# Linear attention and a two-layer network on one core: the query maxima cross the partition groups through a DRAM tile, per token half, where copies within on-chip memory did it per head pair

## The chip, the cores and the metric

The kernel runs on one core of a Trainium2 chip. The metric is device time in microseconds (us) of one execution. The kernel before has a median of 1189.84 us over three runs (1189.03 to 1190.34).

The core has five engines, each with its own queue of instructions that it takes strictly in order: TensorE (PE; its weight loads are listed as PEld), VectorE (DVE), ScalarE (ACT), GpSimd (POOL) and SyncE (SP), which here only issues DMAs. An instruction that waits holds up all that stands behind it on its engine.

## The reference

```python
def phi(x):
    proj = np.einsum('bhsd,df->bhsf', x, w_phi)
    proj = proj - np.max(np.abs(proj), axis=-1, keepdims=True)
    return np.concatenate([np.exp(proj), np.exp(-proj)], axis=-1)
q_p, k_p = (phi(q), phi(k))
kv = np.einsum('bhsf,bhsd->bhfd', k_p, v)
z = np.sum(k_p, axis=2)
num = np.einsum('bhsf,bhfd->bhsd', q_p, kv)
den = np.einsum('bhsf,bhf->bhs', q_p, z)[..., None] + 1e-06
attn = num / den
...
h = x @ w_in            # x: (4608, 512), the attention's output, heads side by side
out = np.maximum(0.01 * h, h) @ w_out
```

There are 8 batches, 8 heads, 576 tokens of 64 numbers; `w_phi` is 64 x 128; the network goes from 512 to 2048 and back. What the change touches is the `max(abs(proj))` of the queries: one number for each token and head, over 128 features.

## The kernel before, in words

**Attention.** Two heads make a pair, and 32 pairs (8 batches of 4) are worked one after the other. The first four have code of their own that the change leaves alone. For the others, `k_phase(i)` makes the 128 x 64 key-value sums of pair i and `q_phase(i)` uses them. Pairs 4 to 7 work in plain float32 (`nat`); from pair 8 on each operand is split into a rounded part and a rest, and each product is made of two or three matmuls. The text below calls `q_phase(i)` "phase i".

**A query phase** handles the pair's 576 tokens in two halves of 288 (u = 0, 1):

- L362 to L365: for each head the projection is made with the features on the 128 partitions and the tokens along the row, in a PSUM tile `a`.
- L366: a DVE transpose in blocks of 32 x 32 moves it to the tile `tq`. Within each block tokens are now on partitions and features along the row. The four partition groups of 32 hold four quarters of the features.
- L368: a reduction gives each partition the maximum over its 32 features, for 18 blocks (2 heads x 9 blocks of 32 tokens). This is a quarter maximum; four of them, 32 partitions apart, must still be joined. This is done after both halves are there: L370 issues three DMAs that copy the groups 1 to 3 to the first 32 partitions (tile `m`), L373 reduces the four, and L375 issues three DMAs that copy the result `mx` back to the groups 1 to 3.
- L381 subtracts the maximum (once per half), L383 transposes back in blocks to `mb` (features on partitions again), L388 and L389 take exp of plus and minus the value on ACT, and L395 and a POOL operation of L72 split it into `qh` and `ql`.
- L404, L406 and L409 are the matmuls with the key-value sums. ACT moves numerator and denominator out (L411, L412; denominator in `dn`), L415 to L419 bring the reciprocals into place on DVE, and POOL multiplies (L421) in the tile `ring`, which holds two batches.

**The network** runs over 18 blocks of 256 tokens. `layer1` (L595, L596, L598) makes a slice of 128 hidden features in the PSUM tile `h`; ACT applies the slope (L602) and rounds (L67), POOL makes the rest (L72); `layer2` (L615 to L617) adds the slice to two PSUM tiles `acc`. At a block's end DVE or ACT copies it out and SP stores it (L623). A block can start only when all heads of its tokens are in `ring`. `load_weights` prepares the network's weights on ACT and DVE (L172 to L186) in the first fifth of the run.

**What sets the order.** The code only states priorities. Attention has a higher priority than the network's steps, so a list scheduler puts an attention instruction into an engine's queue as soon as it holds it to be ready, and fills the rest with the network's matmuls. The scheduler's result is a fixed order per engine. A tile takes a buffer of its tag's pool when one is free: `mb` has one, `dn` has two, `tq` has one. DMAs are issued by SP in its order; an issue waits there until its data are ready and its target is free.

Of the kernel before, what the change touches and what calls it, by code (L numbers as in the profile page):

```python
# [9 lines left out]
F32 = mybir.dt.float32  # L10
# [4 lines left out]
ALU = mybir.AluOpType  # L15
AX = mybir.AxisListType

P = 128
# [3 lines left out]
U = 288  # L22
# [22 lines left out]
def attention_moe_kernel(ctx: ExitStack, tc: tile.TileContext, q, k, v, vt, w_phi, w_in, w_out, out):  # L45
    nc = tc.nc
    cp = ctx.enter_context(tc.tile_pool(name="cp", bufs=1))
    sp = ctx.enter_context(tc.tile_pool(name="sp", bufs=1))
    ps = ctx.enter_context(tc.tile_pool(name="ps", bufs=1, space=bass.MemoryType.PSUM))

    def ct(shape, dt, name):
        return cp.tile(shape, dt, tag=name, name=name)

    def st(shape, dt, tag, name=None):
        return sp.tile(shape, dt, tag=tag, name=name or tag, bufs=BUFS.get(tag, 1))
# [18 lines left out]
    def pt(tag):  # L74
        return ps.tile([P, 512], F32, tag=tag, name=tag, bufs=PBUFS[tag])
# [259 lines left out]
    def blocks(x):  # L335
        return x.rearrange("p a b -> p (a b)").rearrange("p (c d) -> p c d", d=32)

    def q_phase(i):
# [13 lines left out]
            wq = w_phi_split()  # L352
            wq_h, wq_l = wq[:, 0], wq[:, 1]
        tq = st([P, 2, 2, U], F32, "tq")
        m = st([P, 4, 2, 18], F32, "mb", "m")
        for u in range(2):
            us = slice(U * u, U * u + U)
            for j in range(2):
                pq = pt("a")[:, 0:U]
                if nat:  # L360
                    r = slice(64 * j, 64 * j + 64)
                    nc.tensor.matmul(pq, lhsT=bd[r, F * j : F * j + F], rhs=rq[r, us], start=True, stop=True)  # L362
                else:
                    nc.tensor.matmul(pq, lhsT=wq_h, rhs=qs[:, j, us], start=True, stop=False)  # L364
                    nc.tensor.matmul(pq, lhsT=wq_l, rhs=qs[:, j, us], start=False, stop=True)  # L365
                nc.vector.transpose(tq[:, u, j], pq)  # L366
                yield
            nc.vector.tensor_reduce(m[:, 0, u], blocks(tq[:, u]), axis=AX.X, op=ALU.max, apply_absolute_value=True)  # L368
        for a in range(1, 4):
            nc.sync.dma_start(m[0:32, a], m[32 * a : 32 * a + 32, 0])  # L370
        yield
        mx = st([P, 2, 18], F32, "mx")
        nc.vector.tensor_reduce(mx[0:32], m[0:32].rearrange("p a u c -> p u c a"), axis=AX.X, op=ALU.max)  # L373
        for a in range(1, 4):
            nc.sync.dma_start(mx[32 * a : 32 * a + 32], mx[0:32])  # L375
        yield
        kvh, kvl = kvs_of[i]
        for u in range(2):
            us = slice(U * u, U * u + U)
            tu = blocks(tq[:, u])  # L380
            nc.vector.tensor_tensor(tu, tu, mx[:, u].unsqueeze(2).broadcast_to([P, 18, 32]), op=ALU.subtract)  # L381
            mb = st([P, 2, U], F32, "mb")
            nc.vector.transpose(mb.rearrange("p a b -> p (a b)"), tq[:, u].rearrange("p a b -> p (a b)"))  # L383
            yield
# [14 lines left out]
            dn = st([P, U], F32, "dn")  # L399
# [158 lines left out]
    def attention():  # L558
        for i in range(NP, B * NP + 1):
            gens = [k_phase(i)] if i < B * NP else []  # L560
            if i > NP:
                gens.append(q_phase(i - 1))
            if i == NN:
                for _ in range(5):
                    next(gens[1])
                    yield i - 1
            while gens:
                for it in list(gens):
                    if next(it, end) is end:
                        gens.remove(it)  # L570
                    else:
                        yield i - 1
            yield i
# [137 lines left out]
```

## Time and profile before

| | us |
|---|---|
| median of three runs | 1189.84 |
| the profiled execution, its own time | 1187.94 |
| its span, first to last instruction | 1186.2 |
| PE busy in it | 1153.7 (97%) |
| DVE busy | 769.2 (65%) |
| ACT busy | 861.3 (73%) |
| POOL busy | 632.7 (53%) |

The page of the profile gives for each group of instructions the line, the engine, the operation, the tiles it writes and reads, the count, the busy time and the mean length, then the idle time of the engine just before them and what ended it. A view of waits lists "who <- whom: us in total, times, longest". A timeline gives the start, the length and the instruction. Views of windows give the busy time of each engine in a stretch. All times in them are from the start of the span. The granted clock of PE was 1.00 throughout.

### The profile page before, as it was taken

How to read it: one execution, taken by the hardware profiler on the slowest of the kernel's cores; microseconds unless marked ns; L12 is line 12 of the kernel's file. 1: busy time of each engine (PE TensorE's matmuls, PEld its weight loads, DVE VectorE, ACT ScalarE, POOL GpSimd, SP SyncE). 2: the span in 40 equal slices, each digit the busy share in tenths (PEclk: the TensorE clock that was granted, in tenths of full speed). 3: DMA queues.
4: the chain of work that ended last, by engine and by line, in shares of the span. 5: the costliest groups of instructions: out<-in, count | busy, mean ns of one | idle time of the engine just before them, and what ended most of it. 6: DMA issues, size and time to landing. Idle time of an engine off the chain costs nothing.

```text
span 1186.2 us, 21604 instructions
## 1 busy us (share of the span) xinstructions
PE 1153.7 (97%) x7496; PEld 1026.5 (87%) x7496; DVE 769.2 (65%) x1326; ACT 861.3 (73%) x2266; POOL 632.7 (53%) x709
## 2 busy tenths in 40 slices
PE   8899999899998999999999999999999999999998
PEld 5677778799887989889999999999999989899997
DVE  5988995587788778777777777757777765200000
ACT  5978775878788778777888878868887785433232
POOL 0131222576576667666666666757666666433232
PEclk9999999999999999999999999999999999999999
DMA  8436331211111111111111111101111100000000
GB/s 218 135 91 168 103 108 36 70 41 34 51 33 50 34 34 29 42 34 30 52 33 51 33 51 26 48 23 40 33 50 34 40 3 20 1 19 9 10 19 18
DMA packets 71005, 57.88 MB, mean 49 GB/s; under 512 B 53232, under 2 KB 54512, under 8 KB 70896
## 3 DMA queue, kind: packets, MB, share of 16 engines
q1 hardware_dynamic: 70896, 56.51, 17.1%
q8 instruction: 59, 0.97, 0.3%
q14 instruction: 50, 0.41, 0.1%
HBM read 46.27 MB, written 9.44 MB: 47 GB/s over the span
## 4 chain that ended last, share of the span: by engine, by line
PE 47%; DVE 2%; DMA 1%; issue 0%; ACT 0%; POOL 0%; SPq 0%; DVEq 0%; ACTq 0%; POOLq 0%
PE h L598 6%; PE h L596 6%; PE h L595 6%; PE acc L616 6%; PE acc L617 6%; PE acc L615 6%; PE c L228 3%; PE a L409 1%; PE a L404 1%; PE a L406 1%; PE a L251 1%; PE a L365 1%; PE a L364 1%; DVE tq L381 0%; DMA mx<-mx 0%
## 5 line engine op out<-in xcount | busy, mean ns | idle before, releaser
L72 POOL TENSOR_TENSOR gl<-g,gh 128x256 fp32r<-128x256 f32 x288 | 237.3, 827 | 305.4 <-ACT gh L67 220.2
L595 PE MATMUL h<-xh,w0h 128*128 128x256 f32 x1088 | 278.8, 283 | 2.4 <-ACT xh L67 1.3
L596 PE MATMUL h<-xh,w0l 128*128 128x256 f32 x1088 | 276.6, 281 | 0.0
L595 PEld LDWEIGHTS h<-xh,w0h 128*128 128x128 f32 x1088 | 205.4, 189 | 12.4 <-ACT g L602 2.4
L615 PE MATMUL acc<-w1h,gh 128*128 128x512 f32 x544 | 214.3, 394 | 0.2 <-DVE o L69 0.2
L616 PE MATMUL acc<-w1l,gh 128*128 128x512 f32 x544 | 213.3, 392 | 0.0
L596 PEld LDWEIGHTS h<-xh,w0l 128*128 128x128 f32 x1088 | 205.3, 189 | 8.4 <-issue 0.4
L617 PE MATMUL acc<-w1h,gl 128*128 128x512 f32 x544 | 203.5, 395 | 2.6 <-POOL rv L198 1.2
L598 PE MATMUL h<-xl,w0h 128*128 128x256 f32 x1088 | 191.2, 281 | 0.0
L602 ACT ACTIVATE g<-h 128x256 f32<-128x256 f32 x288 | 108.3, 381 | 106.0 <-PE h L598 83.0
L72 POOL TENSOR_TENSOR ql<-eq,qh 128x576 fp32r<-128x576 f32 x96 | 142.9, 1500 | 53.3 <-DVE qh L395 44.3
L67 ACT CAST gh<-g 128x256 fp32r<-128x256 f32 x288 | 115.2, 403 | 63.0 <-PE acc L616 60.9
L598 PEld LDWEIGHTS h<-xl,w0h 128*128 128x128 f32 x1088 | 155.9, 188 | 0.9 <-issue 0.4
L72 POOL TENSOR_TENSOR kpl<-ek,kph 128x512 fp32r<-128x512 f32 x72 | 101.5, 1410 | 75.9 <-ACT kph L67 59.3
L617 PEld LDWEIGHTS acc<-w1h,gl 128*128 128x128 f32 x544 | 99.5, 188 | 19.5 <-POOL rv L198 1.4
L69 DVE COPY o<-acc 128x512 f32<-128x512 f32 x17 | 11.7, 688 | 161.0 <-DMA out_dram<-o 118.0
L615 PEld LDWEIGHTS acc<-w1h,gh 128*128 128x128 f32 x544 | 102.5, 188 | 12.1 <-DVE o L69 0.4
L616 PEld LDWEIGHTS acc<-w1l,gh 128*128 128x128 f32 x544 | 102.3, 188 | 11.7
L282 ACT ACTIVATE ek<-pmk,m 128x128 f32<-128x128 f32 (+1 forms) x240 | 89.5, 390 | 13.5 <-DVE m L259 13.1
L281 ACT ACTIVATE ek<-pmk,m4n 128x128 f32<-128x128 f32 (+1 forms) x240 | 90.1, 392 | 8.6 <-DVE m4n L265 3.9
L395 DVE TENSOR_REDUCE qh<-eq 128x576 fp32r<-128x576 f32 x96 | 69.0, 751 | 25.7 <-ACT eq L389 22.9
L256 DVE TENSOR_TENSOR pmk<-a,pmk 128x256 f32<-128x256 f32 (+1 forms) x120 | 49.6, 420 | 54.0 <-ACT pmk L67 52.0
(183 smaller groups left out, 2404.8 us busy)
## 6 DMA issues: line engine op xcount, KB each, us to landing
out_dram<-o SPq DMA_DIRECT2D x36, 256.0 KB, 2.1
rq<-in_q_dram SPq DMA_DIRECT2D x28, 288.0 KB, 2.9
rk<-in_k_dram SPq DMA_DIRECT2D x27, 288.0 KB, 2.8
rv<-in_v_dram SPq DMA_DIRECT2D x29, 256.0 KB, 3.5
ring<-in_w_in_dram SPq DMA_DIRECT2D x9, 512.0 KB, 3.7
f<-in_w_out_dram SPq DMA_DIRECT2D x7, 512.0 KB, 3.6
f<-in_w_in_dram SPq DMA_DIRECT2D x7, 512.0 KB, 3.6
ring<-in_w_out_dram SPq DMA_DIRECT2D x5, 512.0 KB, 3.8
```

The source lines that it names most:

```text
L67: nc.scalar.copy(o, i)
L72: (nc.vector if pick(key) == "v" else nc.gpsimd).tensor_tensor(o, a, b, op=op)
L281: nc.scalar.activation(ek[r, j, 0:F], pmk[r, h], AF.Exp, bias=m4n[r, h : h + 1])
L282: nc.scalar.activation(ek[r, j, F:256], pmk[r, h], AF.Exp, scale=-1.0, bias=m4[r, h : h + 1])
L395: nc.vector.tensor_reduce(qh, eq.unsqueeze(3), axis=AX.X, op=ALU.max)
L595: nc.tensor.matmul(ph, lhsT=weight(0, "h", ft)[:, d * P : d * P + P], rhs=xh[d], start=d == 0, stop=False)
L596: nc.tensor.matmul(ph, lhsT=weight(0, "l", ft)[:, d * P : d * P + P], rhs=xh[d], start=False, stop=False)
L598: nc.tensor.matmul(ph, lhsT=weight(0, "h", ft)[:, d * P : d * P + P], rhs=xl[d], start=False, stop=d == NP - 1)
L602: nc.scalar.activation(g, ph, AF.Prelu, alpha=0.01)
L615: nc.tensor.matmul(a, lhsT=gh[:, ts], rhs=weight(1, "h", ft), start=ft == 0, stop=False)
L616: nc.tensor.matmul(a, lhsT=gh[:, ts], rhs=weight(1, "l", ft), start=False, stop=False)
L617: nc.tensor.matmul(a, lhsT=gl[:, ts], rhs=weight(1, "h", ft), start=False, stop=ft == NFT - 1)
```

## The change

Each half of a phase now joins its own quarter maxima. The half's reduction (now L372) writes 18 numbers per partition to a tile `mu`, which takes a buffer of the tag `dn`. One DMA (L374) writes them to a DRAM tile `md` of 256 rows of 18 numbers, twice: rows 0 to 127 and again rows 128 to 255. A second DMA (L375) reads them back so that partition p gets the rows p, p + 32, p + 64 and p + 96, side by side; these reads overlap each other. A reduction over the four (L383) then runs on all 128 partitions, in the loop over the halves, just ahead of the subtraction (L384). The three DMAs each way, the reduction on 32 partitions and the tile `mx` are gone. DMAs per phase: four in place of six; joining reductions on DVE: two in place of one. The read waits on SP for the write to land.

```diff
+    dp = ctx.enter_context(tc.tile_pool(name="dp", bufs=1, space=bass.MemoryType.DRAM))
...
-        m = st([P, 4, 2, 18], F32, "mb", "m")
+        m = []
         for u in range(2):
...
-            nc.vector.tensor_reduce(m[:, 0, u], blocks(tq[:, u]), axis=AX.X, op=ALU.max, apply_absolute_value=True)
-        for a in range(1, 4):
-            nc.sync.dma_start(m[0:32, a], m[32 * a : 32 * a + 32, 0])
-        yield
-        mx = st([P, 2, 18], F32, "mx")
-        nc.vector.tensor_reduce(mx[0:32], m[0:32].rearrange("p a u c -> p u c a"), axis=AX.X, op=ALU.max)
-        for a in range(1, 4):
-            nc.sync.dma_start(mx[32 * a : 32 * a + 32], mx[0:32])
+            mu = st([P, U], F32, "dn", "m")
+            mx, mr = mu[:, 0:18], mu[:, 36:108].rearrange("p (a c) -> p a c", c=18)
+            nc.vector.tensor_reduce(mx, blocks(tq[:, u]), axis=AX.X, op=ALU.max, apply_absolute_value=True)
+            md = dp.tile([8 * 32, 18], F32, tag="md", name="md", bufs=4)
+            nc.sync.dma_start(md.rearrange("(r p) c -> p r c", r=2), mx.unsqueeze(1).broadcast_to([P, 2, 18]))
+            nc.sync.dma_start(mr, bass.AP(md.tensor, md.offset, [[18, P], [32 * 18, 4], [1, 18]]))
+            m.append(mu)
         yield
         kvh, kvl = kvs_of[i]
         for u in range(2):
             us = slice(U * u, U * u + U)
             tu = blocks(tq[:, u])
-            nc.vector.tensor_tensor(tu, tu, mx[:, u].unsqueeze(2).broadcast_to([P, 18, 32]), op=ALU.subtract)
+            mt, mr = m[u][:, 18:36], m[u][:, 36:108]
+            nc.vector.tensor_reduce(mt, mr.rearrange("p (a c) -> p c a", c=18), axis=AX.X, op=ALU.max)
+            nc.vector.tensor_tensor(tu, tu, mt.unsqueeze(2).broadcast_to([P, 18, 32]), op=ALU.subtract)
             mb = st([P, 2, U], F32, "mb")
```

The lines behind the change move by two or three numbers: the subtraction L381 is now L384, the transpose L383 is L386, the split L395 is L398, the first numerator matmul L404 is L407.

Since the scheduler sees other instructions, the order changes on every engine from phase 4 on. Three places follow. First SP at the end of the attention (phases 29, 30 and 31), before the change; `out_dram` rows are the network's stores, `rq` is the load of the next pair's queries.

```order
L370 DMA m<-m 32x36 x3
L203 DMA rq<-in_q_dram 128x576
L623 DMA out_dram<-o 128x512
L375 DMA mx<-mx 32x36 x3
L623 DMA out_dram<-o 128x512
L370 DMA m<-m 32x36 x3
L375 DMA mx<-mx 32x36 x3
L370 DMA m<-m 32x36 x3
L623 DMA out_dram<-o 128x512
L375 DMA mx<-mx 32x36 x3
```

The same phases on SP after the change; `md<-m` is the write to DRAM, `m<-md` the read.

```order
L374 DMA md<-m 128x2x18
L375 DMA m<-md 128x4x18
L205 DMA rq<-in_q_dram 128x576
L374 DMA md<-m 128x2x18
L375 DMA m<-md 128x4x18
L626 DMA out_dram<-o 128x512 x2
L374 DMA md<-m 128x2x18
L375 DMA m<-md 128x4x18
L374 DMA md<-m 128x2x18
L375 DMA m<-md 128x4x18
L374 DMA md<-m 128x2x18 x2
L375 DMA m<-md 128x4x18 x2
```

Each half has a write and a read of its own; in phase 31 both writes stand ahead of both reads, and no store of the network stands between them any more.

Second, DVE in phase 31, the last, before the change: from the transposes of the projections to the first split of the exponentials.

```order
L366 STREAM_TRANSPOSE tq<-a 128x288 x2
L368 TENSOR_REDUCE m<-tq 128x18
L366 STREAM_TRANSPOSE tq<-a 128x288
L368 TENSOR_REDUCE m<-tq 128x18
L373 TENSOR_REDUCE mx<-m 32x36
L69 COPY o<-acc 128x512
L381 TENSOR_TENSOR tq<-tq,mx 128x576 x2
L383 STREAM_TRANSPOSE mb<-tq 128x576
L395 TENSOR_REDUCE qh<-eq 128x576 x2
```

The same place after the change; `kvl` belongs to the key phase.

```order
L368 STREAM_TRANSPOSE tq<-a 128x288 x2
L372 TENSOR_REDUCE m<-tq 128x18
L368 STREAM_TRANSPOSE tq<-a 128x288
L372 TENSOR_REDUCE m<-tq 128x18
L332 TENSOR_TENSOR kvl<-c,kvh 128x4x64
L333 TENSOR_TENSOR kvl<-c,kvh 128x4x64
L383 TENSOR_REDUCE m<-m 128x18
L384 TENSOR_TENSOR tq<-tq,m 128x576
L383 TENSOR_REDUCE m<-m 128x18
L386 STREAM_TRANSPOSE mb<-tq 128x576
L384 TENSOR_TENSOR tq<-tq,m 128x576
L398 TENSOR_REDUCE qh<-eq 128x576 x2
```

The first half's subtraction no longer stands behind the second half's share of the join, but the second half's joining reduction stands ahead of the first half's transpose.

Third, DVE in phase 5, where the network's weights are prepared between the query's rows (`ql`, `w0l`, `w1l`; `w0l` and `w1l` are the rests of the two weight matrices). Before the change, from the joining reduction, which stands some way behind both halves' maxima, to the subtractions.

```order
L373 TENSOR_REDUCE mx<-m 32x36
L183 ISA ql<-ql,kvl 128x1024
L178 TENSOR_SCALAR ql<-ql 128x512
L179 TENSOR_SCALAR ql<-ql 128x512
L180 SCALAR_TENSOR_TENSOR ql<-f_79,ql 128x512
L72 TENSOR_TENSOR w0l_818<-ql,w0h_817 128x512
L183 ISA ql<-ql,kvl 128x1024
L178 TENSOR_SCALAR ql<-ql 128x512
L179 TENSOR_SCALAR ql<-ql 128x512
L72 TENSOR_TENSOR w1l_831<-ql,w1h_830 128x512
L180 SCALAR_TENSOR_TENSOR ql<-ring,ql 128x512
L381 TENSOR_TENSOR tq<-tq,mx 128x576 x2
```

After the change, from the first half's own maxima to its subtraction; `pmk` and `m` with a number belong to the key phase.

```order
L372 TENSOR_REDUCE m<-tq 128x18
L74 TENSOR_TENSOR w1l_833<-ql,w1h_832 128x512
L185 ISA ql<-ql,kvl 128x1024
L261 TENSOR_REDUCE m_1251<-a 128x4
L180 TENSOR_SCALAR ql<-ql 128x512
L264 TENSOR_TENSOR pmk<-a,m_1251 128x512
L74 TENSOR_TENSOR w0l_820<-ql,w0h_819 128x512
L181 TENSOR_SCALAR ql<-ql 128x512
L368 STREAM_TRANSPOSE tq<-a 128x288
L383 TENSOR_REDUCE m<-m 128x18
L182 SCALAR_TENSOR_TENSOR ql<-f_84,ql 128x512
L384 TENSOR_TENSOR tq<-tq,m 128x576
```

The first half is joined and subtracted before the second half has its maxima; eight rows stand between its maxima and its join, seven of them work of the weights or the keys. On PE the counts between a phase's first-half projections and its first numerator matmul go, with the median over phases 8 to 31, from 127 matmuls to 105; counted from the second half's projections, from 105.5 to 82.5.

## The prediction, made before the changed kernel ran

> **What bounds the kernel now.** I read the page's first rows, then PE's stretches, then the waits of PE, then the timeline of the last query phase. The first section of the page gives busy time per engine:
>
> ```profile
> span 1186.2 us, 21604 instructions
> PE 1153.7 (97%) x7496; PEld 1026.5 (87%) x7496; DVE 769.2 (65%) x1326; ACT 861.3 (73%) x2266; POOL 632.7 (53%) x709
> ```
>
> PE is the bound: 1186.2 - 1153.7 = 32.5 us of the span are not PE. The matmuls stay the same in kind and number, so all that the change can win or lose on PE is the size of its gaps. Where they lie is in the view of windows (stretch, length, then busy time and instructions of PE, PEld, DVE, ACT, POOL; clock, DMA share, GB/s):
>
> ```profile
> 100.00:150.00 50.00, 48.66 (x270) 38.00 (x269) 46.44 (x83) 38.29 (x87) 11.57 (x15) 1.00 0.42 118
> 600.00:650.00 50.00, 50.00 (x348) 46.44 (x347) 38.55 (x67) 43.48 (x118) 32.82 (x33) 1.00 0.15 43
> 85.00:240.00 155.00, 148.93 (x850) 119.05 (x849) 121.42 (x218) 117.48 (x290) 45.56 (x62) 1.00 0.33 94
> 240.00:1020.00 780.00, 768.74 (x5255) 705.72 (x5255) 577.38 (x968) 628.31 (x1699) 518.20 (x539) 1.00 0.13 36
> ```
>
> The phases that the change touches run from about 85 to 1020 us. There PE lacks 155.00 - 148.93 = 6.1 us and 780.00 - 768.74 = 11.3 us, 17.3 us in all: that is the most that any change here can win. At 600 to 650 us PE has no gap and passes 50.00 / 348 = 0.144 us per matmul, my rate for cover. Which gaps belong to the query's chain is in the waits of PE (who <- whom: us, times, longest):
>
> ```profile
> PE a L404 <- DVE qh L395: 3.9, 4, 1.4
> PE a L404 <- DVE pmk L256: 1.6, 1, 1.6
> PE a L404 <- ACT eq L388: 0.5, 1, 0.5
> ```
>
> L404 is the numerator's first matmul, the end of the chain projection, maxima, exchange, subtraction, exp. Three rows, 6.0 us of the 17.3; the other gaps wait for the network's or the keys' own work. The worst is in phase 31. Its timeline on DVE, SP and PE (start, length, line):
>
> ```profile
> 997.48 0.71 DVE L368 TENSOR_REDUCE m<-tq 128x18 f32<-128x576 f32 x1
> 998.63 0.75 DVE L368 TENSOR_REDUCE m<-tq 128x18 f32<-128x576 f32 x1
> 1002.53 0.41 DVE L373 TENSOR_REDUCE mx<-m 32x36 f32<-32x144 f32 x1 [3.16 <-DMA m<-m]
> 1007.93 1.97 DVE L381 TENSOR_TENSOR tq<-tq,mx 128x576 f32<-128x576 f32 x2 [3.59 <-DMA mx<-mx]
> 1009.82 0.77 DVE L383 STREAM_TRANSPOSE mb<-tq 128x576 f32<-128x576 f32 x1
> 1011.43 1.42 DVE L395 TENSOR_REDUCE qh<-eq 128x576 fp32r<-128x576 f32 x2 [0.84 <-ACT eq L389]
> 999.45 1.77 SPq L370 DMA_DIRECT2D m<-m  x3
> 1002.97 1.78 SPq L375 DMA_DIRECT2D mx<-mx  x3
> 996.57 0.29 PE L365 MATMUL a<-qs,wq 128*128 128x288 f32 x1
> 1012.24 0.40 PE L404 MATMUL a<-qh,kvh 128*128 128x288 f32 x1 [1.45 <-DVE qh L395]
> ```
>
> From the second half's maxima (999.38) to the subtraction (1007.93) the exchange takes 8.55 us, while DVE stands still for 3.16 and 3.59 us, and PE then waits 1.45 us.
>
> **The change part by part.**
>
> *What goes.* Six DMAs and L373. In an undisturbed phase (18) the exchange reads, on DVE:
>
> ```profile
> 571.82 0.75 DVE L368 TENSOR_REDUCE m<-tq 128x18 f32<-128x576 f32 x1
> 576.13 0.41 DVE L373 TENSOR_REDUCE mx<-m 32x36 f32<-32x144 f32 x1
> 579.57 1.43 DVE L381 TENSOR_TENSOR tq<-tq,mx 128x576 f32<-128x576 f32 x2 [0.31 <-DMA mx<-mx]
> ```
>
> From 572.57 to 579.57 are 7.0 us, and it cannot start before the second half is reduced.
>
> *What comes.* A write and a read through DRAM. No row shows either; the nearest are the DMA rows (KB each, median us from issue to landing):
>
> ```profile
> out_dram<-o SPq DMA_DIRECT2D x36, 256.0 KB, 2.1
> rv<-in_v_dram SPq DMA_DIRECT2D x29, 256.0 KB, 3.5
> rv<-in_vt_dram SPq DMA_DIRECT2D x58, 32.0 KB, 2.9
> m<-m SPq DMA_DIRECT2D x84, 4.5 KB, 1.7
> mx<-mx SPq DMA_DIRECT2D x84, 4.5 KB, 1.7
> f<-in_v_dram SPq DMA_DIRECT2D x3, 256.0 KB, 3.8
> wr<-in_w_phi_dram SPq DMA_DIRECT2D x2, 32.0 KB, 2.1
> ```
>
> The write carries 256 pieces of 72 bytes: between the on-chip copy (1.7) and the store (2.1); I take 1.9. The read carries 512 pieces of 72 bytes, 36 KB: between `wr` (2.1, 64 rows of 512 bytes) and `rv` (3.5, 1024 pieces of 256 bytes), nearest to `wr` in bytes and between `vt` and `rv` in pieces; I take 2.6. The trip is then 1.9 + 2.6 = 4.5 us, bounds 3.8 and 5.6. The one thing that no row bounds is the size of a piece written to DRAM: the stores here have rows of 2 KB. The Trainium skill (DMA: Bandwidth & Descriptors, Specifications) says that a transfer below 512 bytes is done as a read-modify-write; no run here shows it; by an estimate from that page, with the 0.2 us per HBM access of its section Latency and other measured facts and 16 pieces on each DMA engine one after the other, the write would take 3.2 us longer, the trip 7.7 us, and, priced as the rival below, the sum would be +14 us in place of -2.9.
>
> *Joining.* L383 reduces 72 numbers to 18 per partition. Rows:
>
> ```profile
> L418 DVE RECIPROCAL rc<-dn 128x9 f32<-128x9 f32 x56 | 12.0, 214 | 1.6
> L373 DVE TENSOR_REDUCE mx<-m 32x36 f32<-32x144 f32 x28 | 11.2, 401 | 9.2 <-DMA m<-m 9.0
> ```
>
> Between 0.21 (9 numbers) and 0.40 us (144): 0.3. DVE gets 56 x 0.3 - 11.2 = +5.6 us. It is 65% busy and not the bound; its cover is gone only where it is full (100 to 150 us: 46.44 of 50). SP issues 112 DMAs in place of 168; an issue takes 1.77 / 3 = 0.59 us, so SP gains 33 us, off the path.
>
> *The chain.* A half now needs 4.5 + 0.3 = 4.8 us where both together needed 7.0, and the first half starts from its own maxima. PE, for its part, now passes 105 matmuls between the first half's last projection and L404 (median, by the order), where 105.5 stood between the second half's and L404. So the cover is the same 105 x 0.144 = 15.1 us and the chain under it is 7.0 - 4.8 = 2.2 us shorter. The longest of the four waits for `qh` was 1.4 us, so all four go: -3.9 us. The wait of 0.5 us for `eq` is in phase 4, where 87 matmuls now cover in place of 82: -0.5. The 1.6 us behind `pmk` wait for key work on DVE: I leave them.
>
> Checked on phase 31: first maxima at 998.19; trip to 1002.7, join to 1003.0, subtraction 0.84 to 1003.8. The second write goes out at 999.4 and its read behind the first read, so the second join, which stands ahead of the first transpose on DVE, can run at about 1003.9 and ends at 1004.2. Transpose 0.77, exp 0.84 (the gap before L395) and the split's half of 1.42 give 1006.5. PE has 76 matmuls from 996.7: 10.9 us, to 1007.6. L404 is ready 1.1 us early, and 1.45 us go.
>
> *The new wait.* L383 waits for the read's landing with key work or the weights' preparation behind it on DVE; ACT's exp and PE's L404 wait for those. SP holds the read until the write has landed; behind it are the next pair's loads, needed a whole phase later. DVE's waits for the exchange so far (us, times, longest):
>
> ```profile
> DVE tq L381 <- DMA mx<-mx: 15.1, 11, 3.6
> DVE mx L373 <- DMA m<-m: 9.0, 11, 3.2
> ```
>
> 24.1 us cost PE only the gaps above; I expect 10 to 30 us of such waits again, hidden by DVE's spare 35%. `m` moves from the tag `mb` to the two buffers of `dn`: a half's denominator must wait for the other half's maxima to be used. That is one subtraction, hidden while L404 is not late; if that cover is gone, it is one subtraction of 0.84 us per phase.
>
> *The early stage.* In phases 5, 6 and 7 the order leaves 51, 67 and 60 matmuls before L404 in place of 113, 83 and 76 (from the second half's projections), and DMA is at 0.42. With the trip's upper bound of 5.6 us phase 7 needs 1.6 (projection to maxima, as 996.6 to 998.2) + 5.6 + 0.3 + 0.84 + 0.77 + 0.84 = 10.0 us, and any DVE row that stands between comes on top; 60 matmuls pass 8.6 us at 0.144 and 10.8 us at the stage's own 48.66 / 270 = 0.18. I charge 1.5 us for the stage, with 0 and 6 (2 us in each of three phases) as ends.
>
> **Sum.** -3.9 - 0.5 + 1.5 = -2.9 us. The profiled execution took 1187.94 us, 1.7 around its span of 1186.2; the median of the runs is 1.9 above that. Against the profiled execution 1185.0, against the median 1189.84 - 2.9 = **1186.9 us**.
>
> **The rivals.**
>
> *Gaps are only dealt again.* Every queue is reordered from phase 4 on. The other 11.3 us of gaps (17.3 - 6.0) are chance meetings of an in-order PE with work a little late; they can come out 3 us worse as well as better, and eat the gain. For it: the gaps' longest are 1.6 us and have many releasers. Against: the query chain has the largest row. Time: 1189.8.
>
> *Small writes to DRAM are slow* (slower). If the trip takes 4.5 + 2.2 = 6.7 us, the advantage is gone; beyond, each phase is late. As bounds stand the slowest landing of a copy of `mx` (the view of that tile; 3.7) and the median of the first loads of `v` (3.8, above):
>
> ```profile
> DMA to landing us min/median/max: 1.6/1.7/3.7
> ```
>
> Together 7.5 us, 0.8 too long: up to 28 x 0.8 = 22 us if no phase has spare, 0 if each has; the middle is +11: 1200.8. For it: pieces of 72 bytes. Against: the copies' pieces of 144 bytes land in 1.7. By the skill's read-modify-write rule it would come out here.
>
> *The early stage has no cover* (slower). 6 us lost in phases 5 to 7 where I charge 1.5: -4.4 + 6 = +1.6, and with weights late behind a waiting DVE, 46.44 of 50 busy, about as much again: +4: 1193.8. For it: the counts. Against: of these 50 us PE so far idles 1.34.
>
> **How the numbers follow.** Forecast 0.47, gaps dealt again 0.27, slow writes 0.14, early stage 0.12. A measurement can tell 0.2%, 2.4 us, from no change. The forecast's own spread, -7 (some of the other gaps go too) to -1, lies mostly beyond -2.4: 0.37 of its 0.47; of the second case 0.06 is faster, 0.17 the same, 0.04 slower. The slower cases give 0.21 slower and 0.05 the same. Faster 0.43, same 0.32, slower 0.25. Range: 1182.8 to 1196.0, from the forecast's low end past the early stage's 1193.8 to the lower half of slow writes.
>
> **What would show it.** Right: the row "L404 <- qh" under 1.5 us, the write landing in 1.7 to 2.1, the read in 2.1 to 3.0, PE's gap from 240 to 1020 us near 7 us. Wrong: a write over 3 us; DVE waits for the read over 40 us in all; PE's gap from 85 to 240 us above 9 us.

## The result, and the profile after

The changed kernel has a median of 1198.87 us over four runs (1197.17 to 1201.06), the kernel before 1189.43 over four in the same comparison (1188.57 to 1190.34). The ratio is 1.0083, 95% interval 1.0068 to 1.0098. I had forecast 1186.9 and a range up to 1196.0: the change costs 9 us where I expected a gain of 3.

The page of the kernel after begins:

```profile
span 1195.4 us, 21620 instructions
PE 1154.9 (97%) x7496; PEld 1028.6 (86%) x7496; DVE 752.6 (63%) x1354; ACT 859.0 (72%) x2266; POOL 626.1 (52%) x709
```

PE has the same matmuls and is nearly as busy as before (1154.9 against 1153.7), so 8.0 of the 9.2 us that the span has grown are gaps. The windows show where (columns as in the prediction):

```profile
85.00:240.00 155.00, 148.30 (x829) 117.08 (x828) 115.66 (x216) 116.64 (x285) 44.47 (x61) 1.00 0.35 93
240.00:1020.00 780.00, 761.34 (x5220) 701.49 (x5219) 567.62 (x1001) 625.07 (x1700) 510.02 (x536) 1.00 0.16 39
```

From 240 to 1020 us PE lacks 18.7 us in place of 11.3, from 85 to 240 us 6.7 in place of 6.1. The waits of PE name the place:

```profile
PE a L407 <- DVE qh L398: 10.8, 10, 2.1
PE h L598 <- ACT g L605: 5.6, 8, 1.7
```

The wait for `qh`, which was to vanish, has grown from 3.9 us in four to 10.8 us in ten. Yet the transfers cost what I said. From the page's DMA issues (KB each, median us to landing):

```profile
m<-md SPq DMA_DIRECT2D x56, 36.0 KB, 2.0
md<-m SPq DMA_DIRECT2D x56, 18.0 KB, 2.0
```

And the join, from the groups by line:

```profile
L383 DVE TENSOR_REDUCE m<-m 128x18 f32<-128x72 f32 x56 | 15.7, 280 | 32.3 <-DMA m<-md 32.0
```

The trip takes 2.0 + 2.0 = 4.0 us (forecast 4.5), the join 0.28 (0.3). What stands behind it on DVE is in the timeline of phase 18 after, from the first half's maximum to its splits:

```profile
557.67 0.74 DVE L372 TENSOR_REDUCE m<-tq 128x18 f32<-128x576 f32 x1
...
564.67 0.29 DVE L383 TENSOR_REDUCE m<-m 128x18 f32<-128x72 f32 x1 [1.06 <-DMA m<-md]
564.99 1.09 DVE L384 TENSOR_TENSOR tq<-tq,m 128x576 f32<-128x576 f32 x1
...
566.34 0.76 DVE L386 STREAM_TRANSPOSE mb<-tq 128x576 f32<-128x576 f32 x1
567.03 0.38 DVE L258 TENSOR_TENSOR pmk<-a,pmk 128x256 f32<-128x256 f32 x1
567.34 0.26 DVE L383 TENSOR_REDUCE m<-m 128x18 f32<-128x72 f32 x1
567.52 0.67 DVE L261 TENSOR_REDUCE m<-pmk 128x4 f32<-128x512 f32 x1
568.12 0.74 DVE L384 TENSOR_TENSOR tq<-tq,m 128x576 f32<-128x576 f32 x1
568.78 0.15 DVE L267 TENSOR_SCALAR m4n<-m 128x4 f32<-128x4 f32 x1
568.97 2.52 DVE L218 TENSOR_TENSOR ks<-rk,ks 64x576 fp32r<-64x576 f32 x2
571.52 1.41 DVE L398 TENSOR_REDUCE qh<-eq 128x576 fp32r<-128x576 f32 x2
```

The first half is transposed back at 567.1, but its splits start at 571.5: six rows (seven instructions) stand between, the next pair's key work (`pmk`, `m` of L261, `m4n`, `ks`) and the second half's join and subtraction. ACT had the exponentials ready (start, length, line):

```profile
567.17 0.45 ACT L391 ACTIVATE eq<-mb 128x288 f32<-128x288 f32 x1
567.52 0.43 ACT L392 ACTIVATE eq<-mb 128x288 f32<-128x288 f32 x1
```

So the first split's input was there at 567.95, 3.6 us early, and PE waits:

```profile
572.42 0.37 PE L407 MATMUL a<-qh,kvh 128*128 128x288 f32 x1 [1.20 <-DVE qh L398]
```

In phase 18 before the change, such key work ran while the exchange was on its way (it ended at 579.57), and nothing stood between the transposition and the split, which waited for ACT alone:

```profile
574.17 0.76 DVE L256 TENSOR_TENSOR pmk<-a,pmk 128x256 f32<-128x256 f32 x2
...
576.65 0.75 DVE L216 TENSOR_TENSOR ks<-rk,ks 64x576 fp32r<-64x576 f32 x1
...
580.92 0.78 DVE L383 STREAM_TRANSPOSE mb<-tq 128x576 f32<-128x576 f32 x1
583.53 0.75 DVE L395 TENSOR_REDUCE qh<-eq 128x576 fp32r<-128x576 f32 x1 [1.83 <-ACT eq L389]
```

Over phases 8 to 31, 5.9 instructions stand there on the mean after the change, in a stretch of 4.0 us; before it was 0.25 in 0.9 us. That gave me my first theory: DVE's order is the cause. Its rivals were the trip through DRAM, and a new deal of every queue by chance. None of the three survived the runs as it stood. A deal is, here and below, one outcome of the scheduler: the same work in another order.

### The profile page after: what moved, and what is told of

Read it like the earlier page. It is cut to its first block, busy times and chain, and to the rows that moved or that the text cites. A ratio compares the mean times of both kernels' runs of the same rounds, so it can differ in the third digit from the quotient of the medians.

```text
span 1195.4 us, 21620 instructions
## 1 busy us (share of the span) xinstructions
PE 1154.9 (97%) x7496; PEld 1028.6 (86%) x7496; DVE 752.6 (63%) x1354; ACT 859.0 (72%) x2266; POOL 626.1 (52%) x709
## 4 chain that ended last, share of the span: by engine, by line
PE 55%; DVE 17%; ACT 11%; DMA 8%; issue 5%; POOL 3%; SPq 1%; POOLq 0%; DVEq 0%; ACTq 0%
PE h L598 7%; PE h L599 7%; PE h L601 7%; PE acc L618 7%; PE acc L620 7%; PE acc L619 7%; PE c L230 4%; DMA m<-md 3%; DVE ks L218 3%; DMA md<-m 3%; PE a L407 2%; DVE tq L384 2%; PE a L412 2%; PE a L409 2%; DVE qs L349 1%
## 5 line engine op out<-in xcount | busy, mean ns | idle before, releaser
L74 POOL TENSOR_TENSOR gl<-g,gh 128x256 fp32r<-128x256 f32 x288 | 230.6, 804 | 309.1 <-ACT gh L69 245.6
L74 POOL TENSOR_TENSOR kpl<-ek,kph 128x512 fp32r<-128x512 f32 x72 | 98.9, 1373 | 61.1 <-ACT kph L69 52.6
L619 PEld LDWEIGHTS acc<-w1l,gh 128*128 128x128 f32 x544 | 102.6, 189 | 12.5
L283 ACT ACTIVATE ek<-pmk,m4n 128x128 f32<-128x128 f32 (+1 forms) x240 | 91.3, 394 | 23.5 <-DVE m4n L267 15.2
L398 DVE TENSOR_REDUCE qh<-eq 128x576 fp32r<-128x576 f32 x96 | 71.0, 751 | 34.4 <-ACT eq L392 13.1
L368 DVE STREAM_TRANSPOSE tq<-a 128x288 f32<-128x288 f32 x112 | 51.7, 469 | 35.4 <-PE a L367 31.9
```

The source lines that it names most:

```text
L74: (nc.vector if pick(key) == "v" else nc.gpsimd).tensor_tensor(o, a, b, op=op)
L283: nc.scalar.activation(ek[r, j, 0:F], pmk[r, h], AF.Exp, bias=m4n[r, h : h + 1])
L398: nc.vector.tensor_reduce(qh, eq.unsqueeze(3), axis=AX.X, op=ALU.max)
L619: nc.tensor.matmul(a, lhsT=gh[:, ts], rhs=weight(1, "l", ft), start=False, stop=False)
```

## The experiments

The text on record speaks of "the changed kernel" and "before"; its theory A is DVE's order, B the trip, C the chance of the deal. Times are medians, each ratio is to runs of before on the same chip.

### Is it the trip?

Four kernels. *no_exchange* is the changed kernel with no trip at all:

```diff
-            md = dp.tile([8 * 32, 18], F32, tag="md", name="md", bufs=4)
-            nc.sync.dma_start(md..., mx...)
-            nc.sync.dma_start(mr, bass.AP(md.tensor, ...))
...
-            mt, mr = m[u][:, 18:36], m[u][:, 36:108]
-            nc.vector.tensor_reduce(mt, mr..., axis=AX.X, op=ALU.max)
+            mt = m[u][:, 0:18]
```

> Left out: the exchange of the maxima; each partition group subtracts its own quarter maximum (no write, no read, no joining reduction). Theory A (the queue on DVE): the numerator's matmul waits because rows of other work stand between the transpose back and the first split on DVE (5.9 per phase after, 0.25 before); here they are 5.4, and the matmuls between the first half's projection and the numerator fall from 105 to 86. So PE's wait for qh stays at 8 us or more and the time at 1193 or more, though there is no trip at all. Theory B (the trip through DRAM is on the path): without a trip the waits for qh fall below 3 us and the time to 1188 or less. Theory C (only re-dealt gaps): anything from 1185 to 1200, with no relation to the rows between.

1205.51 us, ratio 1.0133 (1.0108 to 1.0157). Slower still, without any trip; theory A had the time but not the wait for `qh`, which it put at 8 us or more. PE's waits:

```profile
PE c L230 <- DVE kvl L333: 10.1, 8, 3.4
...
PE acc L616 <- POOL gl L74: 3.7, 7, 0.8
PE a L403 <- DVE qh L394: 3.7, 8, 0.8
```

The trip cannot be the cause. The loss has moved to the keys' matmuls and the network's.

*long_trip* copies the read's result once more on chip before the join:

```diff
+            nc.sync.dma_start(mr, mu[:, 108:180].rearrange("p (a c) -> p a c", c=18))
```

> The changed kernel with one more DMA on chip behind the read, about 1.7 us plus its issue, per token half. Theory A: the scheduler knows of the hop and moves PE's numerator back (110.5 matmuls of cover in place of 105); the rows between stay at 5.2, so the waits for qh stay near 10 us and the time within 3 us of the changed kernel's 1198.9. Theory B: each half is 2.3 us later, the waits for qh rise above 18 us and the time to 1206 or more. Theory C: no relation, 1190 to 1202.

1213.36 us, ratio 1.0197 (1.0173 to 1.0222); `qh` 13.0 us in 11 waits. A longer trip costs too: the time is what theory B asked for (1206 or more), though the wait for `qh` is not (over 18 us), and theory A, which had it within 3 us of the changed kernel, missed by 11.

*phase_dram* goes through DRAM once per phase, both halves together, with `m` in the tag `mb` as before:

```diff
-            mu = st([P, U], F32, "dn", "m")
+        m = st([P, U], F32, "mb", "m")
...
+        md = dp.tile([8 * 32, 36], F32, tag="md", name="md", bufs=4)
+        nc.sync.dma_start(md..., m[:, 0:36]...)
+        nc.sync.dma_start(mr..., bass.AP(md.tensor, md.offset, [[36, P], [32 * 36, 4], [1, 36]]))
+        yield
+        nc.vector.tensor_reduce(m[:, 36:72], mr..., axis=AX.X, op=ALU.max)
```

> The exchange through DRAM, but once per phase for both halves as in the kernel before (one write, one read, one joining reduction on 128 partitions, the maxima in the tag mb). Theory A: the rows between fall to 2.7 per phase, so the waits for qh are between those of before (3.9) and after (10.8), and the time 1190 to 1195. Theory B: the trip through DRAM is there once per phase, on the path of both halves: waits for qh of 9 us or more, 1197 or more. Theory C: 1186 to 1200.

1192.69 us, ratio 1.0033 (1.0018 to 1.0049), and PE's gaps add up to 24.4 us, as before (24.3).

*half_chip* does the opposite: exchange per half, but with before's on-chip copies, three each way (`m` in `dn`):

```diff
-        for a in range(1, 4):
-            nc.sync.dma_start(m[0:32, a], m[32 * a : 32 * a + 32, 0])
+            for a in range(1, 4):
+                nc.sync.dma_start(m[0:32, a], m[32 * a : 32 * a + 32, 0])
+            nc.vector.tensor_reduce(m[0:32, 4], m[0:32, 0:4]..., axis=AX.X, op=ALU.max)
```

> Per token half as in the changed kernel, but on chip: three DMAs to the first 32 partitions, a reduction there, three DMAs back, no DRAM; twice as many DMAs as before. Theory A: rows between 2.2 per phase, waits for qh 4 to 9 us, 1190 to 1195. Theory B: no DRAM trip, but two on-chip trips of 7 us: as before, 1188 to 1191, unless the doubled issues on SP (12 x 0.59 us per phase) come onto the path. Theory C: 1186 to 1200.

1197.56 us, ratio 1.0066 (1.0045 to 1.0087), more than A or B allowed. So the way does not decide, on chip or through DRAM: one exchange per phase stays near before, one per half is slower.

### Is it the order of rows on DVE?

*second_late* queues the second half's join and subtraction behind the first half's last split:

```diff
+            with tc.issue_after(ls.ins) if ls is not None else nullcontext():
-            nc.vector.tensor_reduce(mt, ...)
+                nc.vector.tensor_reduce(mt, ...)
```

> The changed kernel, but on DVE the second half's join and subtraction are queued behind the first half's last split into qh, so they can no longer stand between the first half's transposition back and its split. By the order, 5.0 rows of other work still stand there per phase (5.9 in the changed kernel): two rows of the second half go, and rows of key work take part of their place. DVE's order as the cause: the row 'L407 <- qh' shrinks from 10.8 to 4 to 9 us and the time falls by 1 to 5 us, to 1193 to 1198. Only re-dealt gaps: no relation, 1190 to 1205. The trip through DRAM as the cause: the trip stays, so the time stays at 1197 to 1201.

1213.33 us, ratio 1.0201 (1.0178 to 1.0224). A miss: `qh` is at 9.9 us in 18 waits, and the numerators' gaps for all reasons rise from 13.7 to 18.2.

*both_first* puts both joins ahead of the first subtraction:

```diff
+        for u in range(2):
+            lj = nc.vector.tensor_reduce(mt, ...)
         for u in range(2):
+            with tc.issue_after(lj.ins):
```

> The changed kernel with its transfers per half through DRAM as they are, but on DVE both joins stand ahead of the first subtraction: the halves meet again, as before the change. By the order, 3.3 rows of other work stand between transposition and split (5.9 in the changed kernel, 0.3 before), and PE has 113 matmuls between the first half's projection and its numerator (105 and 127). DVE's order as the cause: the row 'L407 <- qh' under 6 us and a time of 1189 to 1194. Only re-dealt gaps: no relation, 1188 to 1205. The trip through DRAM as the cause: the time stays at 1197 to 1201, with the row above 8 us.

1209.24 us, ratio 1.0152 (1.0130 to 1.0174), `qh` 13.0 us. Also a miss, by 15 us: fewer rows in between, and more waiting.

Both edits made the scheduler deal every queue anew, so I next held the orders: edges between consecutive instructions of an engine, taken from the finished program, with one engine's order edited.

```diff
+        for x, y in zip(order, order[1:]):
+            tc.add_manual_dep(ins[f"I-{y}"], f"I-{x}", mybir.DependencyInfo(...NoSync...), reason="order")
```

So every other row stays where it is in the changed kernel.

*split_early* moves the first half's splits on DVE up to its transposition back:

> The changed kernel with every engine's order held as it is there, but on DVE the two splits into qh of each split phase's first half stand directly behind its transposition back; the 5.9 rows that stood between come behind them. Nothing else moves. DVE's order as the cause: those rows were what made qh late, 'L407 <- qh' falls under 3 us, and the time to 1189 to 1193. Slack as the cause: the same gain at qh, but DVE now waits 0.8 to 1.7 us for exp in front of the splits with the key work behind it, which comes late: half or more is lost at the keys' rows, 1193 to 1199. Only re-dealt gaps: 1196 to 1206.

1247.96 us, ratio 1.0481 (1.0459 to 1.0504). PE's waits:

```profile
PE h L598 <- ACT g L605: 18.5, 12, 3.0
PE c L230 <- ACT kph L69: 11.0, 6, 3.4
PE c L230 <- DVE kvl L333: 6.6, 2, 3.4
...
PE a L407 <- DVE qh L398: 3.1, 3, 2.1
```

The time is far above what any of the three theories had (1206 at most). Half of mine holds: the rows in between were what made `qh` late, 10.8 goes to 3.1. But put behind the splits, they make the keys' matmuls and the network's wait: PE's gaps at key matmuls go from 4.4 to 21.0 us, at the network's from 8.3 to 33.3.

*numer_late* moves only the numerators on PE, behind up to 8 of the network's matmuls that follow:

> The changed kernel with every engine's order held as it is there, but on PE each split phase's numerators stand later, behind up to 8 of the network's matmuls that follow them (6 on the mean for the first half, 0.9 us at 0.144; other attention matmuls are not passed). Nothing else moves. Slack as the cause (PE reaches the numerators earlier than the chain is ready): the row 'L407 <- qh' falls from 10.8 to under 5 us, PE's gaps by 5 to 8 us, and the time to 1190 to 1195. DVE's order as the cause: the same rows stand between transposition and split, but the numerators come later, so it gains too, 2 to 6 us. Only re-dealt gaps: what is won at qh comes back at other rows, 1196 to 1202.

1200.51 us, ratio 1.0072 (1.0052 to 1.0091; the changed kernel's is 1.0083). Its profiled execution took 1205.8 us:

```profile
PE h L598 <- ACT g L605: 7.4, 11, 1.6
PE a L407 <- DVE qh L398: 5.3, 8, 1.5
```

The wait for `qh` halves, and the time is unchanged, though slack and DVE's order had both promised a gain: gaps at the numerators fall from 13.7 to 7.0 us, those at the keys and the network rise by 4.8 together, and 3.4 us more are lost to half clock (last section).

### Whose gain is it?

Two kernels exchange PE's orders, with one yield added or taken away (below) so that the tiles are taken in the same sequence; the other engines' orders are the scheduler's. *pe_as_after* is the kernel before with PE's order of the changed kernel:

> The kernel before (with one yield less, for the same reason) with PE's order held as it is in the changed kernel; exchange on chip, other engines' orders the scheduler's. The numerators now stand 22 matmuls, 3.2 us, earlier over a chain that is as long as before (slack of 1.4 us in the median): about 1.8 us late in each of 24 phases. 0.7 rows stand on DVE between transposition and split. Slack as the cause: 24 x 1.8 = 43 us in the worst case, some of it taken up by the next phase's later start: the rows 'L404 <- qh' or 'eq' over 20 us, 1205 to 1235. DVE's order as the cause: 0.7 rows, 1188 to 1194. Only re-dealt gaps: as the changed kernel, 1195 to 1202.

1290.99 us, ratio 1.0843 (1.0825 to 1.0861):

```profile
PE a L403 <- DVE qh L394: 57.2, 22, 4.9
PE a L403 <- ACT eq L387: 26.2, 4, 8.8
```

Worse than the upper bound, but of the kind that the slack theory named. The old exchange cannot serve the numerators where the change has put them: the shorter trip is real, and in the change's order it is spent on earlier numerators.

*pe_as_before* is the changed kernel with PE's order of before:

> The changed kernel (with one more yield, so that the tiles are taken in the order of before) with PE's order held as it is in the kernel before, matmul by matmul; the other engines' orders are the scheduler's for that. Transfers and joins are those of the change, so the chain under the old cover is shorter by the trip's 4 us. By the order 127 matmuls cover the first half (105 in the changed kernel), but 7.2 rows of other work stand on DVE between transposition and split. Slack as the cause: 'L407 <- qh' under 2 us, PE's gaps 18 to 24 us, 1182 to 1190. DVE's order as the cause: 7.2 rows, so 'L407 <- qh' at 8 us or more and 1195 to 1202. Only re-dealt gaps: the other queues are dealt anew, 1190 to 1205.

1271.75 us, ratio 1.0678 (1.0653 to 1.0703):

```profile
PE c L230 <- POOL kpl L74: 27.9, 16, 2.8
PE c L230 <- ACT kph L69: 22.7, 14, 5.8
```

`qh` is gone from the list, as the slack theory said, but the time is 82 us above before, where that theory had 1190 at most. The query chain is now ready 7.4 us before its numerator, and the key chain, which shares DVE, ACT and POOL with it, is late. Whether other orders of those three would serve both wasn't tried.

### Is it the chance of the deal?

`k_phase` and `q_phase` are generators that run in turn; a `yield` is where the other goes on. Yields add no work, they change the sequence in which the scheduler sees the same instructions. *before_y12* lacks the two around the exchange of before:

```diff
             nc.sync.dma_start(m[0:32, a], m[32 * a : 32 * a + 32, 0])
-        yield
...
             nc.sync.dma_start(mx[32 * a : 32 * a + 32], mx[0:32])
-        yield
```

> The kernel before with two yields fewer around the exchange, nothing else: the attention's steps are dealt in another order, and the exchange on chip stays. By the order 0.04 rows stand between transposition and split (0.25 before), and 126 matmuls cover the first half (127). DVE's order as the cause: within 3 us of before, 1187 to 1193, 'L404 <- qh' under 5 us. Only re-dealt gaps: a new deal alone moves the time by 3 to 10 us, to 1192 or more or 1186 or less, with other rows of PE's waits than before.

1194.72 us, ratio 1.0044 (1.0029 to 1.0060). *after_y0* takes the one behind `m.append(mu)` from the changed kernel:

> The changed kernel with one yield fewer, between the halves' maxima and the joins, nothing else. By the order 3.8 rows stand between transposition and split (5.9 in the changed kernel), 1.7 of them the second half's join and subtraction; the key rows halve. PE has 99 matmuls of cover for the first half and 73 for the second (105 and 82.5). DVE's order as the cause: the rows are fewer but the cover is shorter by 6 to 10 matmuls, 0.9 to 1.4 us, so 'L407 <- qh' stays at 8 to 14 us and the time at 1195 to 1201. Only re-dealt gaps: anything from 1188 to 1206, with the loss at other rows. The trip through DRAM as the cause: 1197 to 1201.

1207.14 us, ratio 1.0142 (1.0127 to 1.0157). A deal is thus worth 5 to 7 us, which made chance the likeliest theory. Four more deals: *before_more_yields* has one more behind before's exchange, *before_fewer_yields* none behind L383's transpose, *after_one_more* and *after_two_more* have one and two more behind `m.append(mu)`.

> The kernel before with one yield more behind its exchange, nothing else: a new deal of the same work. Chance of the deal: a new deal alone moves the time by as much as the change did, so among the deals of before at least one comes out at 1197 or more (two were 1189.4 and 1194.7 so far), and the deals of both exchanges overlap. A cost of the exchange per half beyond chance: every deal of before stays at 1188 to 1196, below every deal of the change.

1191.38 us, ratio 1.0004 (0.9991 to 1.0018).

> The kernel before without the yield behind each half's transposition back, nothing else: another new deal of the same work. Chance of the deal: 1187 to 1205, overlapping with the deals of the change. A cost of the exchange per half beyond chance: 1188 to 1196.

1186.06 us, ratio 0.9962 (0.9950 to 0.9974): this beats both kernels.

> The changed kernel with one yield more between the halves' maxima and the joins, as the kernel before has: a new deal, about a tenth of the rows change place. Chance of the deal: 1190 to 1208, as likely under 1197 as over it. A cost of the exchange per half beyond chance: 1197 or more, as the two deals of the change so far (1198.9 and 1207.1).

1203.85 us, ratio 1.0112 (1.0091 to 1.0134).

> The changed kernel with two yields more at the same place: a third new deal of the change, with a third of the rows moved. Chance of the deal: 1190 to 1208. A cost of the exchange per half beyond chance: 1197 or more.

1202.02 us, ratio 1.0098 (1.0077 to 1.0120).

Four deals of before lie at ratios from 0.9962 to 1.0044, mean 1.0003; four of the change from 1.0083 to 1.0142, mean 1.0109. They do not overlap. Chance is worth some 4 us either way; between the two means lie 1.06%, about 12.6 us.

### The tag, or the exchange per half?

All slow kernels so far had `m` in `dn`. *phase_dram_dn* is phase_dram with `m` in `dn`:

```diff
-        m = st([P, U], F32, "mb", "m")
+        m = st([P, U], F32, "dn", "m")
```

> phase_dram (one trip through DRAM per phase, 1192.7) with its tile m in the tag dn in place of mb, nothing else. In the change m stands in dn too, whose two buffers the denominators need: there a phase's maxima wait for the previous phase's last denominator, and its first denominator for the maxima to be used. The shared tag as the cost: 4 us or more over phase_dram, 1197 to 1206. The exchange per half as the cost (twice the transfers and joins): no change beyond a new deal, 1187 to 1196. The first half's early start as the cost: the same, 1187 to 1196.

1185.66 us, ratio 0.9961 (0.9949 to 0.9973): faster than both kernels, with the trip through DRAM and with the shared tag. The gain is no larger than what a deal is worth: with phase_dram the mean ratio is 0.9997. Its waits of PE and its transfers:

```profile
PE a L405 <- DVE qh L396: 7.3, 11, 2.0
...
PE h L596 <- ACT g L603: 2.1, 3, 1.2
```

```profile
m<-md SPq DMA_DIRECT2D x28, 72.0 KB, 2.1
...
md<-m SPq DMA_DIRECT2D x28, 36.0 KB, 1.9
```

*half_mb* is the changed kernel with both halves' `m` in one tile of `mb`:

```diff
+        mm = st([P, U], F32, "mb", "m")
...
-            mu = st([P, U], F32, "dn", "m")
+            mu = mm[:, 108 * u : 108 * u + 108]
```

> The changed kernel with both halves' maxima in one tile of the tag mb in place of two of dn; transfers and joins per half as in the change. mb has one buffer, so both subtractions now stand ahead of the first transposition back, as in phase_dram. The shared tag as the cost: as the deals of before, 1187 to 1196. The exchange per half as the cost: as the deals of the change, 1198 to 1207. The first half's early start as the cost: 1187 to 1196 too, but the kernel with both joins ahead of the first subtraction, in dn, took 1209, which speaks against it.

1198.66 us, ratio 1.0075 (1.0050 to 1.0100), with

```profile
PE a L408 <- DVE qh L399: 10.2, 11, 2.4
```

The tag is not the cost; taking the halves apart is. The six kernels that join per phase lie at 1185.7 to 1194.7 us, the nine that join per half, in orders of the scheduler's (two with edges of mine), at 1197.6 to 1213.4, whatever the way, the tag or the trip's length. no_exchange, at 1205.5, has neither transfers nor joins and loses too, so their number is not the cost either.

### All runs side by side

PE's gaps of the profiled executions in us, sorted by the matmul that ends them; "all" holds the first four pairs and the query projections too, but not the wait for the first matmul. "Lost clock" is half of the time at half clock, without the drop behind the last work. "Slack" is the mean time from the first half's `qh` to its numerator, phases 8 to 31. These are sums of mine over the trace's records. In pe_as_after a few late numerators lift the mean slack; in 21 of its 24 phases the numerator waits.

| kernel | us | numerators | keys | network | all gaps | lost clock | slack |
|---|---|---|---|---|---|---|---|
| before | 1189.4 | 6.4 | 4.4 | 6.5 | 24.3 | 0 | 1.24 |
| before_y12 | 1194.7 | 7.6 | 6.6 | 3.1 | 25.1 | 5.1 | 1.63 |
| before_more_yields | 1191.4 | 2.2 | 7.6 | 6.3 | 22.5 | 3.4 | 1.28 |
| before_fewer_yields | 1186.1 | 3.3 | 4.5 | 5.9 | 20.1 | 0 | 1.19 |
| phase_dram | 1192.7 | 7.3 | 6.5 | 4.0 | 24.4 | 1.7 | 0.88 |
| phase_dram_dn | 1185.7 | 8.7 | 2.0 | 4.2 | 20.2 | 1.7 | 0.78 |
| half_chip | 1197.6 | 5.0 | 6.9 | 11.6 | 29.4 | 1.7 | 1.20 |
| half_mb | 1198.7 | 12.1 | 3.2 | 5.6 | 25.9 | 3.4 | 0.58 |
| **after** | 1198.9 | 13.7 | 4.4 | 8.3 | 32.0 | 1.7 | 0.35 |
| after_y0 | 1207.1 | 10.5 | 9.3 | 10.0 | 34.6 | 5.1 | 0.69 |
| after_one_more | 1203.9 | 13.1 | 4.4 | 9.5 | 32.9 | 3.4 | 0.33 |
| after_two_more | 1202.0 | 10.1 | 5.1 | 11.2 | 32.1 | 3.4 | 0.51 |
| both_first | 1209.2 | 15.2 | 6.6 | 6.3 | 34.9 | 5.1 | 0.46 |
| long_trip | 1213.4 | 18.5 | 7.5 | 10.0 | 41.7 | 6.8 | 0.68 |
| second_late | 1213.3 | 18.2 | 5.5 | 9.4 | 38.6 | 3.4 | 0.50 |
| no_exchange | 1205.5 | 4.0 | 11.2 | 12.5 | 33.5 | 6.8 | 2.38 |
| numer_late | 1200.5 | 7.0 | 7.3 | 10.2 | 32.7 | 5.1 | 0.83 |
| split_early | 1248.0 | 4.8 | 21.0 | 33.3 | 65.2 | 17.1 | 2.99 |
| pe_as_before | 1271.8 | 1.4 | 58.1 | 14.6 | 80.4 | 32.4 | 7.41 |
| pe_as_after | 1291.0 | 84.2 | 0.5 | 4.0 | 94.9 | 46.1 | 1.35 |

For the change the account closes: span +9.2 us = gaps +7.7, lost clock +1.7, and -0.2 left. It does not close for all: half_mb's span is 9.7 us longer than before's and 4.7 of these are left, both_first's 20.8 and 5.1, second_late's 24.9 and 7.2, so the gaps do not tell all of their loss. Means over the four deals: numerators 4.9 before and 11.8 after, keys 5.8 and 5.8, network 5.5 and 9.7, lost clock 2.1 and 3.4.

## Why the prediction was wrong

**The step that failed** is the one on the chain: "the cover is the same 105 x 0.144 = 15.1 us and the chain under it is 7.0 - 4.8 = 2.2 us shorter". The chain under it is 2.2 us longer. Means of phases 8 to 31, from the start of the last projection matmul ahead of the cover (before the second half's, after the first's):

| us | before | after | |
|---|---|---|---|
| projection to its maximum | 2.02 | 3.86 | +1.84 |
| maximum to subtraction | 7.85 | 6.04 | -1.81 |
| subtraction to transposed back | 3.14 | 2.25 | -0.89 |
| transposed back to `qh` | 1.67 | 4.77 | +3.10 |
| sum, to `qh` | 14.69 | 16.93 | +2.24 |
| to the numerator on PE | 15.93 | 17.27 | +1.34 |
| slack | 1.24 | 0.35 | -0.89 |

The term that I worked out, the second line, came near the forecast (-1.8 against -2.2), partly by luck: both its ends are longer than I had them (7.85 and 6.04 for 7.0 and 4.8). The lines that I took as fixed did not stay. I priced the instructions of the chain and left out the rows of other work that an in-order engine has between them; the exchange was the time in which DVE did the keys' work, and a shorter exchange does not make that work less. The order of the changed kernel, which I had before the run, shows these rows; for phases 8 to 31 I counted PE's matmuls in it and not DVE's rows. Nor can they be had back singly: half_mb, with `m` in `mb`, has 2.3 us in the first line, 7.1 in the third and 1.9 in the fourth, with 2.0 rows in place of 5.9 ahead of the split, and is no faster.

**The check on phase 31** held, and misled me. I had its first split done at 1006.5 and its numerator's input 1.1 us early. After the change, on DVE and then on PE:

```profile
1004.62 0.77 DVE L386 STREAM_TRANSPOSE mb<-tq 128x576 f32<-128x576 f32 x1
1005.32 0.95 DVE L384 TENSOR_TENSOR tq<-tq,m 128x576 f32<-128x576 f32 x1
1006.24 1.42 DVE L398 TENSOR_REDUCE qh<-eq 128x576 fp32r<-128x576 f32 x2
```

```profile
1008.05 0.29 PE L407 MATMUL a<-qh,kvh 128*128 128x288 f32 x1
```

The first of the two splits is done at about 1006.9, PE comes at 1008.05 and does not wait: the 1.45 us are gone. But phase 31 is the last: there is no pair 32, so no next pair's key phase runs beside it. I had tested the mechanism on the one phase of 28 without the thing that broke it.

**The other terms.** Write and read are 2.0 each (I took 1.9 and 2.6); the join is 0.28. DVE waits 32.0 us for the read, just over my 10 to 30. The early stage's gaps grew by 0.6, where I charged 1.5. The shared tag, which I called hidden, delays the first maximum (where PE's order is the scheduler's, it ends 2.2 to 2.3 us after its projection with `mb`, 2.7 to 4.7 with `dn`), but phase_dram_dn (2.7) is not slower for it, nor half_mb (2.3) faster.

**The rivals.** "Small writes to DRAM are slow" gave 1200.8, next to the measured 1198.9, by a mechanism that isn't there: the trip takes 4.0 us, not the 7.5 that it was priced with. A time that fits proves nothing about its reason. "Gaps are only dealt again" was right that deals move the time, but too small: I allowed 3 us, the four deals of before span 8.7. Of my signs for "right" the write's landing came (2.0), the read's was a little shorter than its 2.1 to 3.0, and the row for `qh` and the gap from 240 to 1020 us did not come. Of my signs for "wrong" (a slow write, long waits of DVE, a gap in the early stage) none came: none named the reason.

**Shown, and open.** Shown: the loss goes with taking the halves apart, not with DRAM, the tag, the number of transfers or chance; the time saved on the trip was turned into numerators 1.9 us earlier (projection to numerator 19.12 us before, 17.27 after, both of the first half) and into key work behind the subtraction; moving either back alone, as split_early and numer_late did, only moves the wait or adds to it. That less slack lets the numerators' gaps grow is argued from the table (slack of 1.2 to 1.6 us and gaps of 2 to 8 in the deals of before, 0.3 to 0.7 and 10 to 14 in those of the change), not shown by a run of its own; half_chip and no_exchange have the slack and lose at the keys and the network. Open is why the scheduler, which fixes the order from its own estimate of all times, leaves less slack with halves than with whole phases: no trace shows that estimate.

## What to carry to other kernels

A wait in an in-order queue is also the time in which that engine's other work gets done; before you shorten it, list what it covers and say where that goes. Test a chain on a phase in the middle, with all its neighbours, not on the one at the end that is easiest to read. Where a scheduler deals the queues, time several neutral deals of both kernels before you believe a difference under 1%, and change one thing at a time: the exchange through DRAM cost nothing that a deal does not (phase_dram and phase_dram_dn, 1192.7 and 1185.7), its split into halves did.

## What the runs showed of the hardware

**The clock drops after short gaps.** In the kernel after, around 448 us (windows as above; the clock is the last column but two):

```profile
440.00:448.40 8.40, 6.08 (x43) 5.20 (x42) 8.09 (x15) 6.97 (x20) 3.23 (x3) 1.00 0.41 106
448.40:451.80 3.40, 3.40 (x14) 3.01 (x14) 2.27 (x4) 1.61 (x4) 3.07 (x4) 0.50 0.21 80
451.80:460.00 8.20, 8.20 (x56) 7.48 (x55) 4.84 (x7) 6.07 (x17) 6.86 (x7) 1.00 0.01 2
```

PE stood still for 2.0 us up to 447.3; from 448.4 on the granted clock is 0.50 for 3.41 us, in which PE does 14 matmuls where 23 fit. That costs 1.7 us, nearly as much as the gap itself. The Trainium skill (TensorE: Matmul & The Clock Gate, What's actually happening) states a free-running window of 3413 ns with half clock after an idle one; the length agrees. But the window need not be idle throughout: I cut the 18 traces that show such drops into windows of 3.413 us on the grid that the drops give. All 56 windows in which PE stood still for 1.91 us or more were followed by half clock, and of 5,713 with under 0.5 us none; at 1.7 to 1.91 us it was 14 of 29, between 0.5 and 1.7 us 20 of 408 (9 of these were at half clock themselves).

**Small pieces in DRAM.** Writes of 256 pieces of 72 bytes land in 2.0 us, as fast as the network's 256 KB stores in before (2.1), and reads of 512 such pieces in 2.0. The Trainium skill (DMA: Bandwidth & Descriptors, Specifications) has transfers under 512 bytes done as read-modify-write; these landings show no price for it.
